# Moving one tile's DMA transposes ahead of the next loads, and its copies of k to other places

## The chip, the cores and the metric

The kernel runs on one core of a Trainium2 chip. The core has five engines that run in parallel, each through its own list of instructions in order: TensorE (PE, with the weight loads PEld beside it), VectorE (DVE), ScalarE (ACT), GpSimd (POOL) and SyncE (SP), which here issues nearly all DMAs. The metric is the device time of one execution in microseconds (us). Lower is better. The kernel before takes 273.0 us, the median of three runs (272.87, 273.00 and 273.41).

## The reference

The program is an attention over chunks of 64 keys, followed by an MLP of two matrix products with an exact GELU between them. Inputs and output are float32.

```python
batch, n_heads, seq, head_dim = 8, 8, 576, 64           # q, k, v
scores = (1 / sqrt(64)) * q_c @ k_c.transpose           # per chunk of 64: q_c, k_c, v_c are (8, 8, 9, 64, 64)
attn   = exp(scores - max) / (sum + 1e-9)
x      = (attn @ v_c), heads side by side               # 4608 tokens x 512
h      = x @ w_in                                       # 512 x 2048
g      = 0.5 * h * (1 + erf(h / sqrt(2)))
out    = g @ w_out                                      # 2048 x 512
```

## The kernel before, in words

**Tiles.** The 4608 tokens are worked in nine tiles of 512. Tile t from 0 to 7 is eight chunks of batch t. Tile 8 is the ninth chunk of all eight batches. While the MLP of tile t runs on TensorE, the attention of tile n = t + 1 is fitted in between, and the loads for tile t + 3 are under way. The loop `for t in range(1, NT)` (L972) sets this up for each t. The constant `T0` (L482) is 3.

**The MLP of a tile.** The first product (`mm1_seven`, L576) makes 16 slots of h. A number in its `order` is one slot made plainly: four 512-column matmuls (L477) and a GELU on ScalarE (L479). Other slots are made in blocks by a scheme with seven products in place of eight (`seven_rows`, L536). The steps p1 to p7 are its products (L551), each of four 256-column matmuls. s11, s12, c22+ are sums or copies between PSUM banks. s12 is `plus(bank["d"], "a")` on VectorE (L555), and the product p4 then accumulates into the same bank d. c11, c12, c22 are GELUs (L559). The scheme needs sums of blocks of x, the four tensor_tensor instructions of `x_sums` (L534): p5 reads the first, p6 the second, p7 the third, p3 the fourth. The second product (`mm2_seven`, L646) also has seven block products, of two half-steps each (14 slots, L706), with sums of blocks of h from `g_sum` (L644 and, for the third, L631).

**The attention of a tile.** q and k arrive in float32 on SP (`load_qk`, L118), GpSimd casts them to bf16 (`pool_cast_qk`, L164), and SP's DMA transposes bring them to the layout that the scores need (`flip`, L194, into q_t and k_t; k_t has one buffer). `k_by_chunk` (L196) then copies k_t in four instructions (L207), one for each pair of heads, to k_c, whose columns stand chunk by chunk; for tile 5 it writes back into that tile's k_nat, which the transpose has read by then. `quad_S` (L233) makes the scores on TensorE (L239) and their exponentials on ScalarE (L246). `quad_sums`, `quad_over`, `att_rc` and `quad_x_plain` form the sums and scale the result of the value product `quad_av` (L334) into x. V is loaded by nine DMAs of a tile on SP (`load_v_rows`, L128) and cast on GpSimd (`cast_v_rows`, L214).

**What sets the order.** Every engine's order is written out by hand. `mm1_seven` walks its `order` list: a step such as "p4" issues its work, and a name or number that has hooks in `extra1` (e1 in the loop) issues those first. `mm2_seven` does the same for its slots with `extra2` (e2). "x" is the place of the x sums and "k" the place of the k copies. `next_loads` (L997) issues, for tile t, the loads and casts of q and k of tile t + 3, and of V of tile t + 2. A DMA on SP waits in line behind all earlier ones, and SP often runs behind the other engines.

In the kernel before, the loop of tile 2 issues `next_loads` first (q and k of tile 5, V of tile 4). The transposes of tile 4 come at the first slot of the second product:

```python
            if t == T0:
                flip(n + 1, "q")
            elif t > 1:
                next_loads()
```

In the loop of tile 3 the copies of tile 4's k stand at "k", behind p3. The transpose of tile 5's k and `next_loads` stand ahead of slot 9, and the copies of tile 5's k (VectorE, all four) ahead of slot 15. The scores of both tile 4 and tile 5 are made in the second product of tile 3 (slots 0 and 10).

Of the kernel before, what the change touches and what calls it, by code (L numbers as in the profile page):

```python
# [11 lines left out]
def kernel(  # L12
# [178 lines left out]
    def flip(t, nm):  # L191
        st = tiles[t]
        st[nm + "t"] = flips.tile([P, G * J, P], bf16, tag=nm + "t", name=f"{nm}_t", bufs=2 if nm == "q" else 1)
        nc.sync.dma_start_transpose(st[nm + "t"][:], st[nm][:].rearrange("p g j r d -> p (g j r d)"))  # L194

    def k_by_chunk(t, copy, gs=range(G)):  # L196

        st = tiles[t]
        if t == K0:
            st["kc"] = st["kt"][:].rearrange("p (g n) (c e) -> p g (n c) e", g=G, c=2)  # L200
            return
        if "kc" not in st and t == T0 + 2:
            st["kc"] = st["k"][:].rearrange("p g j r d -> p (g j r d)").rearrange("p (g i e) -> p g i e", g=G, i=CT)
        elif "kc" not in st:
            st["kc"] = flips.tile([P, G, CT, CH], bf16, tag="kc", name="k_c", bufs=1)
        for g in gs:
            copy(st["kc"][:, g].rearrange("p i (c j) -> p i c j", j=J),  # L207
                 st["kt"][:, g * J:(g + 1) * J].rearrange("p j (i c) -> p i c j", i=CT))
# [108 lines left out]
    def quad_over(t, m):  # L317

        rb, r1 = tiles[t]["rb"], tiles[t]["r1"]
        for s in range(G):  # L320
            nc.scalar.copy(rb[QD * s:QD * (s + 1), m], r1[QD * m:QD * (m + 1), (m % 2) ^ (s // 2)])
# [108 lines left out]
    DV, AC, PO = nc.vector.tensor_copy, nc.scalar.copy, nc.gpsimd.tensor_copy  # L430
# [51 lines left out]
    T0 = 3  # L482
# [93 lines left out]
    def mm1_seven(t, hooks):  # L576

        if t > 1:
            tiles[t]["h"] = hpool.tile([P, FF, MT], bf16, tag="h", name="h")
        kept = [work.tile([P, HM, HD], f32, tag="t1", name="kept_p5", bufs=2)[:] for _ in range(2 if t in TWICE else 1)]  # L580
        bank, more = {}, {}
        if t == 1:
            does = seven_rows(t, 1, {"a": TP, "b": AT, "d": AT}, kept[0], bank)
        else:
            does = seven_rows(t, 0, {"a": AT, "b": AT, "d": AT}, kept[0], bank)
        if t in TWICE:
            does.update((step + "'", do) for step, do in
                        seven_rows(t, 1, {"a": TP, "b": TP}, kept[1], more).items())
            fifth = does["p5'"]
            does["p5'"] = lambda: (more.update(d=bank["b"]), fifth())  # L590
        if t == NT - 1:
            order = ("p1", "s11", "p1'", "s11'", "p5", 8, "p2", "c11", "p6", 9, "s12", "p5'", "p6'", "s12'", 10, "p7", "p4",
                     "c22+", "c12", "c22", "p7'", 11, "p3", "p2'", "c11'", "c22+'", "p4'", "c22'", 12, "c12'", "p3'", 13,
                     "g0", 14, "s3", 15)
        elif t > T0 + 1:
            order = ("p1", "p1'", "s11", "t0", "s11'", 8, "p2", "p2'", "c11", "p5", "p6", "p5'", "p6'", "c11'", "s12", 9, 10,
                     "s12'", "p7", "p4", "c22+", "p7'", "c22+'", "t1", "p4'", "c12", "c22", "p3", 11, "c12'", "c22'", 12, "p3'",
                     13, "g0", 14, "s3", 15)
        elif t == T0 + 1:
            order = (4, 5, 6, "p1", "s11", 7, "p2", "p5", "c11", "p6", 8, "s12", "t0", 9, 10, "p4", "p7", "c12", "c22+",  # L600
                     "t1", 11, "c22", 12, "p3", "g0", 13, "s3", 14, 15)
        elif t == T0:
            order = ("x", "p1", "s11", 4, "p5", "p2", "c11", 5, "p6", "s12", 6, "p4", "p7", "c12", "c22+", 7, "c22", 8, "p3",
                     "k", 9, 10, "s3", 11, 12, 13, "g0", 14, 15)
        elif t == 2:
            order = ("p1", "s11", "p1'", "x", "s11'", 8, "p2", "c11", "p5", 9, "p6", "s12", "p5'", "p6'", "s12'", 10, "p7", 11,
                     "c22+", "c22", "p7'", 12, "p4", "c12", "p3", "c22+'", "p3'", 13, "p4'", "p2'", "k", "c22'", "c11'", "c12'",
                     "g0", 14, 15, "s3")
        else:
            order = (9, "p1", "s11", 10, 11, "w", "p5", "p2", "c11", "p6", 12, "s12", "w0", "p4", "p7", "c12", "c22+", "w1", 13,  # L610
                     "c22", "p3", 14, "g0", "s3", 15)
        for step in order:
            if step in does:
                does[step]()
                continue
            for u in hooks.get(step, ()):
                u()
            if not isinstance(step, str):
                mm1_slot(t, step)
# [187 lines left out]
    def pool_cast_qk(t, names="qk"):  # L807
        for nm in names:
            for g in range(G):
                cast_qk(t, nm, g, PO)  # L810
# [33 lines left out]
    with tc.manual_schedule():  # L844
# [46 lines left out]
        p2 = att_sum_pe(0, 2)  # L891
        p3 = att_sum_pe(0, 3)
# [70 lines left out]
        def flip_qk(t):  # L963
            for nm in "qk":
                flip(t, nm)
# [6 lines left out]
        for t in range(1, NT):  # L972
            n = t + 1
# [35 lines left out]
                    pool_cast_qk(t + 3, "k")  # L1009
            if t == T0:  # L1010
                flip(n + 1, "q")
            elif t > 1:
                next_loads()
            e1, e2 = {}, {}
            exp, gelu = lambda: act_table(Act.Exp), lambda: act_table(Act.Gelu)
# [3 lines left out]
            e1 = {"s3": [lambda: g_sum(t, 3)], "g0": g[0]} if t not in DENSE else {9: [lambda: g_sum(t, 3)], 13: g[0]}  # L1019
            e2 = {0: g[1][:2], 2: g[1][2:]}  # L1020
            if t <= T0:
                ov = [lambda m=m: quad_over(n, m) for m in range(G)]
                rx = [[lambda m=m: att_rc(n, m), lambda m=m: quad_x_plain(n, m)] for m in range(G)]
                e2 = {0: [exp, lambda: quad_S(n, ALONE)] + g[1][:2], 2: g[1][2:],
                      4: [lambda: quad_sums(n)], 5: [ov[0]], 6: [ov[1]],
                      7: [ov[2]] + rx[0], 8: [ov[3]] + rx[1], 9: rx[2], 10: rx[3]}
                e2[{1: 7, 2: 5, T0: 4}[t]].insert(1, lambda: quad_av(n, ALONE))
                if t > 1:
                    e1["x"] = [lambda: x_sums(t)]
                if t == 1:  # L1030
                    e1["w"] = [lambda: weight_sum(2), lambda: weight_sum(3)]
                    e1["w0"] = [lambda: w_in_sums(0, (0, 1))]
                    e1["w1"] = [lambda: w_in_sums(0, (2, 3))]
                    e2[2].append(lambda: weight_sum(4))
                    e2[4].append(lambda: [load_qk(4, nm) for nm in "qk"])
                    e2[7] += [lambda: pool_cast_qk(4), lambda: flip_qk(3), lambda: load_v_rows(3), lambda: cast_v_rows(3, PO)]
                else:
                    e1["k"] = [lambda: k_by_chunk(n, DV)]
                if t < T0:
                    if t > 1:  # L1040
                        e2[0].append(lambda: flip_qk(n + 1))
                    e2[11] = [gelu]
                else:
                    e1[9] = [lambda: flip(n + 1, "k"), next_loads]
                    e1[15] = [lambda: k_by_chunk(n + 1, DV)]
                    e2[10] += [lambda: quad_S(n + 1, BETWEEN), gelu]
                    e2[12] = parts[0]
                    e2[13] = [lambda: x_sums(n)] + parts[1]
            elif n < NT:
                rcs = [lambda m=m: quad_rc(n, m // 2, m % 2) for m in range(G)]  # L1050
                if t == T0 + 1:
                    e1["t0"] = [lambda: quad_total(n, (0,))]
                    e1["t1"] = [lambda: quad_total(n, (1,))] + rcs[1:3]
                else:
                    e1["t0"] = [lambda: quad_totals(n)]
                    e1["t1"] = rcs[1:]
                e2 = {0: [exp, lambda: quad_av(n, ALONE)] + g[1][:2] + xs[:2], 4: xs[2:] + g[1][2:],
                      6: [lambda: x_sums(n, (0, 1))], 10: [lambda: x_sums(n, (2, 3))], 11: [gelu]}
                if t == T0 + 1:
                    e2[2] = rcs[3:]  # L1060
                if n + 1 < NT:
                    for i, gs in enumerate(((0,), (1, 2), (3,))):
                        e2.setdefault(2 * i + 2, []).append(lambda gs=gs: k_by_chunk(n + 1, AC, gs))
                    e2[8] = [lambda: quad_S(n + 1, ALONE)] + parts[0][:1]
                    e2[10] += parts[0][1:] + parts[1]
# [29 lines left out]
```

## Time and profile before

The profile is of one execution on the chip, taken by the hardware profiler. Its times are microseconds from the start of its span.

| what | value |
|---|---|
| median of three runs | 273.0 us (272.87 to 273.41) |
| the profiled execution's own time | 274.27 us |
| its span, first to last instruction | 272.5 us |
| granted TensorE clock | 1.00 |
| TensorE busy | 261.5 us (96%) |
| VectorE busy | 208.1 us (76%) |
| ScalarE busy | 195.1 us (72%) |
| GpSimd busy | 89.6 us (33%) |
| first product of tile 3 | 106.10 to 119.77 |
| second product of tile 3 | 119.77 to 135.35 |

The profiled execution lies 1.27 us over the median. About 1.8 us of its time lie outside the span. An "order of time" below gives start, duration, engine, line, operation, and the tile that is written and the ones that are read; a bracket at the end tells how long the engine was idle before and what ended that. In it the end of a matmul is modelled, and one matmul begins before the one ahead of it has ended, so distances on TensorE are read from start to start. SPq is SP issuing a DMA: its duration is that of the issue, not of the transfer.

### The profile page before, as it was taken

Reading aid. Unit: us, or ns where it says so; the run is one execution under the profiler, and the core shown is the slowest. Engines: PE = TensorE matmul, PEld = TensorE weight load, DVE = VectorE, ACT = ScalarE, POOL = GpSimd, SP = SyncE. Lnnn points to the kernel's source line nnn. Section 1 sums busy time; section 2 is a strip of 40 time slices with the busy share of each in tenths; the row PEclk is TensorE's granted clock in tenths of the full one; section 3 lists DMA queues with packets and bytes.
Section 4 is the critical chain, followed back from the end, with each engine's and each line's share of the span. In section 5 each row is a group of like instructions: output and inputs, shape, how many; then the busy total and the mean of one; then the engine's idle time right before and its main releaser. Section 6 shows DMA issues by size and latency. Waiting matters only on the chain.

```text
span 272.5 us, 7244 instructions
## 1 busy us (share of the span) xinstructions
PE 261.5 (96%) x2913; PEld 192.3 (71%) x2933; DVE 208.1 (76%) x352; ACT 195.1 (72%) x376; POOL 89.6 (33%) x150
## 2 busy tenths in 40 slices
PE   8699999999999999998999999999999999999993
PEld 3378775566876787567855887588758876886682
DVE  6874877989985979578988998888887888635621
ACT  3767758898677967787877967897788779357610
POOL 7869768501284326104534900032400200000000
PEclk9999999999999999999999999999999999999999
DMA  6999999899899897999699327999974220130014
GB/s 206 264 353 404 391 396 227 231 207 250 255 384 229 222 309 173 299 262 286 188 223 349 89 79 186 173 139 166 226 170 99 89 79 2 38 115 2 0 41 117
DMA packets 104738, 53.96 MB, mean 198 GB/s; under 512 B 72960, under 2 KB 101632, under 8 KB 104704
## 3 DMA queue, kind: packets, MB, share of 16 engines
q1 hardware_dynamic: 104400, 53.23, 73.3%
q8 instruction: 23, 0.38, 0.6%
q10 hardware_dynamic: 304, 0.26, 0.3%
q14 instruction: 11, 0.09, 0.1%
HBM read 36.70 MB, written 9.44 MB: 169 GB/s over the span
## 4 chain that ended last, share of the span: by engine, by line
PE 86%; ACT 5%; DMA 4%; SPq 2%; issue 1%; ACTq 0%; DVE 0%; POOL 0%; POOLq 0%
PE y_ps L706 33%; PE h_ps L477 22%; PE hs_ps L551 14%; PE h_ps L451 5%; PE y_ps L778 2%; DMA arrival<-in_moe_w_in_dram 2%; SPq L157 2%; PE av_ps L334 2%; DMA arrival<-in_q_dram 2%; PE h_ps L467 2%; ACT pT L246 1%; PE y_ps L742 1%; PE y_ps L451 1%; PE s_ps L239 1%; ACT L842 1%
## 5 line engine op out<-in xcount | busy, mean ns | idle before, releaser
L477 PE MATMUL h_ps<-x,w_in_sb 128*128 128x512 bf16 x269 | 65.4, 379 | 0.8
L479 ACT ACTIVATE h<-h_ps 128x512 bf16<-128x512 f32 x85 | 50.7, 600 | 19.2 <-PE h_ps L477 14.9
L477 PEld LDWEIGHTS <-w_in_sb 128*128 128x128 bf16 x284 | 27.7, 98 | 25.2
L706 PEld LDWEIGHTS <-h 128*128 128x128 bf16 x384 | 36.9, 98 | 5.0 <-issue 0.2
L164 POOL CAST q_nat<-arrival 128x512 bf16<-128x512 f32 x31 | 20.9, 713 | 58.0 <-DMA arrival<-in_q_dram 32.9
L214 POOL CAST v_nat<-arrival 128x1024 bf16<-128x1024 f32 x14 | 15.2, 1097 | 48.5 <-DMA arrival<-in_v_dram 48.5
L706 PE MATMUL y_ps<-v_bd,k_bd 128*128 128x256 bf16 x256 | 29.8, 273 | 0.8 <-issue 0.7
L706 PE MATMUL y_ps<-w_out_sb,h 128*128 128x256 bf16 x256 | 29.3, 273 | 0.0
L706 PEld LDWEIGHTS <-k_bd 128*128 128x128 bf16 x256 | 24.6, 98 | 4.4 <-issue 0.9
L673 DVE TENSOR_TENSOR kept<-y_ps,kept 128x512 f32<-128x512 f32 (+1 forms) x25 | 16.5, 660 | 12.4 <-PE y_ps L706 8.8
L559 ACT ACTIVATE h<-hs_ps 128x512 bf16<-128x512 f32 x39 | 22.8, 600 | 1.7 <-PE hs_ps L551 1.7
L842 ACT ACT_TABLE_LOAD x18 | 23.1, 1283 | 1.1 <-PEq L1079 0.7
L668 ACT COPY kept<-y_ps 128x512 f32<-128x512 f32 (+1 forms) x26 | 14.5, 557 | 12.7 <-PE y_ps L706 12.5
L164 POOL CAST k_nat<-arrival 128x512 bf16<-128x512 f32 x30 | 19.7, 692 | 7.0 <-DMA arrival<-in_k_dram 6.5
L551 PEld LDWEIGHTS <-w_in_sb 128*128 128x128 bf16 x156 | 15.2, 98 | 5.3 <-issue 0.4
L555 DVE TENSOR_TENSOR hs_ps<-hs_ps,kept_p 128x512 f32<-128x512 f32 x13 | 8.7, 687 | 9.4 <-PE hs_ps L551 7.2
L706 PE MATMUL y_ps<-v_bd,s_sb 128*128 128x256 bf16 x128 | 15.3, 273 | 0.0
L706 PE MATMUL y_ps<-w_out_sb,s 128*128 128x256 bf16 x128 | 15.3, 273 | 0.0
L706 PE MATMUL y_ps<-v_bd,h 128*128 128x256 bf16 x128 | 15.3, 273 | 0.0
L246 ACT ACTIVATE pT<-s_ps 128x512 bf16<-128x512 f32 x28 | 14.4, 603 | 0.7 <-PE s_ps L239 0.7
L451 PE MATMUL h_ps<-x,w_in_sb 128*128 128x256 bf16 x128 | 14.1, 273 | 0.3 <-POOL w_in_sb L823 0.3
L551 PE MATMUL hs_ps<-x,w_in_sb 128*128 128x256 bf16 x104 | 14.3, 273 | 0.0
(138 smaller groups left out, 487.4 us busy)
## 6 DMA issues: line engine op xcount, KB each, us to landing
arrival<-in_v_dram SPq DMA_DIRECT2D x58, 128.0 KB, 4.1
arrival<-in_q_dram SPq DMA_DIRECT2D x7, 1024.0 KB, 7.1
arrival<-in_k_dram SPq DMA_DIRECT2D x6, 1024.0 KB, 10.1
out_dram<-kept SPq DMA_DIRECT2D x21, 256.0 KB, 2.7
arrival<-in_moe_w_out_dram SPq DMA_DIRECT2D x4, 1024.0 KB, 11.6
arrival<-in_moe_w_in_dram SPq DMA_DIRECT2D x6, 512.0 KB, 8.1
out_dram<-y_sb SPq DMA_DIRECT2D x11, 256.0 KB, 2.8
arrival<-in_k_dram SPq DMA_DIRECT2D x8, 256.0 KB, 5.6
```

The source lines that it names most:

```text
L164: copy(st[nm][:, g].rearrange("p j r d -> p r j d"), st[nm + "f"][:, 2 * g:2 * g + 2])
L214: copy(st["v"][:, r::2], st["vf"][:, r::2])
L246: nc.scalar.activation(pT[:].rearrange("p u (c j) -> p u c j", j=J), s_ps[g2][c][:].rearrange("p u (j c) -> p u c j", j=J), Act.Exp, scale ...
L451: nc.tensor.matmul(to[:, cols], left, right[:, cols], start=(start and a == 0), stop=stop, skip_group_check=True)
L477: (nc.tensor.matmul if t else by_halves)(h_ps[:], w_in_sb[:, ks, f * P:(f + 1) * P], tiles[t]["x"][:, ks, :], start=(ks == 0), stop=(ks == ...
L479: nc.scalar.activation(tiles[t]["h"][:, f, :], h_ps[:], Act.Gelu)
L551: nc.tensor.matmul(hs[:, f], left[:, ks, f * P:(f + 1) * P], right[:, ks], start=(fresh and f == 0 and ks == 0), stop=(ks == 1), skip_grou ...
L559: nc.scalar.activation(h[:, n:n + HM, HD * c:HD * (c + 1)], src, Act.Gelu)
L668: nc.scalar.copy(kept[name][:, ms], ps[:])
L673: nc.vector.tensor_tensor(y_sb[:, ms], ps[:], y_sb[:, ms], op=ADD)
L706: nc.tensor.matmul(to, left(f, m), right[:, f], start=(fresh and (split or m == 0) and f == 0), stop=(f == HF - 1), skip_group_check=True)
L842: nc.scalar.activation(act_scratch[:], rest[:, 0:1], func)
```

## The change

In tile 2's loop, the transposes of tile 4's q and k move from the start of the second product to "k" in the first one, behind the copies of tile 3's k, and `next_loads` moves from the start of the loop to the place just behind them. On SP the two transposes thereby stand ahead of the two loads of tile 5's q and k and the nine of tile 4's V; ahead of both stand the same stores as before.

In tile 3's loop, "k" moves from behind p3 to the place right behind "x". So the four copies of tile 4's k follow the x sums on VectorE and stand ahead of s12. The transpose of tile 5's k and `next_loads` also move to that place; on SP their order among the other DMAs stays. The copies of tile 5's k leave slot 15 of the first product. They are issued in slot 2 of the second one, behind the last partial sum: those of heads 4 to 7 on ScalarE, those of heads 0 to 3 on VectorE.

TensorE's and GpSimd's orders stay the same.

```diff
         elif t == T0:
-            order = ("x", "p1", "s11", 4, "p5", "p2", "c11", 5, "p6", "s12", 6, "p4", "p7", "c12", "c22+", 7, "c22", 8, "p3",
-                     "k", 9, 10, "s3", 11, 12, 13, "g0", 14, 15)
+            order = ("x", "k", "p1", "s11", 4, "p5", "p2", "c11", 5, "p6", "s12", 6, "p4", "p7", "c12", "c22+", 7, "c22", 8, "p3",
+                     9, 10, "s3", 11, 12, 13, "g0", 14, 15)
...
             if t == T0:
                 flip(n + 1, "q")
-            elif t > 1:
+            elif t > T0:
                 next_loads()
...
                 else:
-                    e1["k"] = [lambda: k_by_chunk(n, DV)]
+                    e1["k"] = [lambda: k_by_chunk(n, DV), lambda: flip_qk(n + 1) if t < T0 else flip(n + 1, "k"), next_loads]
                 if t < T0:
-                    if t > 1:
-                        e2[0].append(lambda: flip_qk(n + 1))
                     e2[11] = [gelu]
                 else:
-                    e1[9] = [lambda: flip(n + 1, "k"), next_loads]
-                    e1[15] = [lambda: k_by_chunk(n + 1, DV)]
+                    e2[2] += [lambda: k_by_chunk(n + 1, AC, (2, 3))] + [] + [lambda: k_by_chunk(n + 1, DV, (0, 1))]
                     e2[10] += [lambda: quad_S(n + 1, BETWEEN), gelu]
```

## The prediction

> **What bounds the kernel now.** First the page's busy times and its chain that ended last, since they say which engine a microsecond has to be taken from:
>
> ```profile
> PE 261.5 (96%) x2913; PEld 192.3 (71%) x2933; DVE 208.1 (76%) x352; ACT 195.1 (72%) x376; POOL 89.6 (33%) x150
> PE 86%; ACT 5%; DMA 4%; SPq 2%; issue 1%; ACTq 0%; DVE 0%; POOL 0%; POOLq 0%
> ```
>
> TensorE is busy for 261.5 of 272.5 us. No DMA stands on the chain but for the first loads. A transfer or a copy that comes earlier is therefore worth only as much as TensorE waits for it today. Next, the two halves of tile 3, the tile that the change touches most, as stretches (columns: length, then busy time of PE, PEld, DVE, ACT, POOL):
>
> ```profile
> 106.10:119.77 13.67, 13.57 (x77) 7.32 (x77) 9.60 (x15) 10.11 (x18) 3.33 (x4) 1.00 1.07 261
> 119.77:135.35 15.58, 14.88 (x309) 12.69 (x309) 13.41 (x22) 12.46 (x32) 6.60 (x10) 1.00 0.83 237
> ```
>
> In the first product TensorE lacks 0.10 us, in the second 0.70 us. The order of time on TensorE says where:
>
> ```profile
> 109.58 1.03 PE L477 MATMUL h_ps<-x,w_in_sb 128*128 128x512 bf16 x4
> 110.60 0.60 PE L551 MATMUL hs_ps<-x,w_out_sb 128*128 128x256 bf16 x4
> ...
> 127.95 1.58 PE L706 MATMUL y_ps<-v_bd,k_bd 128*128 128x256 bf16 x13 [0.69 <-issue]
> ```
>
> Four 512-column products take 0.86 us from start to start elsewhere (108.28 to 109.14), so p4 at 110.60 starts 0.16 us late. The other gap, 0.69 us, is put down to no engine, semaphore or DMA. So TensorE waits for no transpose and no k copy in tile 3. VectorE does wait for them, as its own order of time shows:
>
> ```profile
> 106.16 0.57 DVE L534 TENSOR_TENSOR k_bd<-x 128x512 bf16<-128x512 bf16 x1
> 106.77 0.72 DVE L534 TENSOR_TENSOR k_bd<-x,k_bd 128x512 bf16<-128x512 bf16 x1
> 107.41 1.25 DVE L534 TENSOR_TENSOR k_bd<-x 128x512 bf16<-128x512 bf16 x1
> 108.58 0.41 DVE L534 TENSOR_TENSOR k_bd<-x,k_bd 128x512 bf16<-128x512 bf16 x1
> 109.84 0.70 DVE L555 TENSOR_TENSOR hs_ps<-hs_ps,kept_p 128x512 f32<-128x512 f32 x1 [0.85 <-PE hs_ps L551]
> 111.67 0.69 DVE L555 TENSOR_TENSOR kept_p<-hs_ps,kept_p 128x512 f32<-128x512 f32 x1 [1.12 <-PE hs_ps L551]
> 113.39 2.14 DVE L207 COPY k_c<-k_t 128x512 bf16<-128x512 bf16 x4 [1.03 <-DMA k_t<-k_nat]
> ```
>
> This is the place that decides. The x sums end at 108.99, and s12 (L555, at 109.84) waited 0.85 us for p6. p4 accumulates into the bank that s12 writes, and p4 starts 0.06 us after s12's end (110.54). So s12 is already on TensorE's path, with 0.85 us of VectorE's idle time ahead of it. The k copies of tile 4 come later, where VectorE is free.
>
> **The change part by part.**
>
> SP, tile 2. Two transposes move ahead of eleven loads: q and k of tile 5 and the nine of tile 4's V. The queue's order of time:
>
> ```profile
> 93.48 0.59 SPq L118 DMA_DIRECT2D arrival<-in_q_dram  x1
> 94.12 0.99 SPq L118 DMA_DIRECT2D arrival<-in_k_dram  x1
> 95.16 12.19 SPq L128 DMA_DIRECT2D arrival<-in_v_dram  x9
> 107.45 1.76 SPq L194 DMA_TRANSPOSE q_t<-q_nat  x1
> 109.32 1.93 SPq L194 DMA_TRANSPOSE k_t<-k_nat  x1
> ```
>
> The casts of tile 4 ended on POOL at 85.3 and the tile-3 copies that free k_t at 89.5, so neither transpose waits at 93.48. They issue at 93.5 and 95.3, and with the 4.0 us from issue to landing of the present k transpose, k_t lands at about 99.4 in place of 113.36. The loads behind them move by 1.76 + 1.93 + two gaps of 0.05 = 3.8 us: q of tile 5 lands at about 104.4 (now 100.64), its k at about 108.4 (now 104.61). Where loads now follow a transpose pair, k lands 10.6 to 12.0 us after the k transpose was issued (138.71 to 149.32; 116.60 to 128.59), which gives 105.9 to 107.3. So k lands between 105.9 and 108.4. V's casts on POOL move from 107.16 and 109.44 to some 111 and 113; the value product that needs them is at 124.34. That costs nothing; without that 10 us of cover, each us would be a us of TensorE.
>
> SP and POOL, tile 3. The transpose of tile 5's k and the loads behind it keep their place on SP: the queue runs behind the program and reaches that transpose at 116.60 now, at some 114 to 117 then. It newly waits only for the early copies of tile 4 to free k_t, by 111.1. No cost. POOL's order is the same.
>
> VectorE, tile 3, k copies of tile 4. Four copies, 0.52 us from start to start (113.39, 113.91), so 2.06 us till the next can start. They move from 113.39 to straight behind the x sums; behind them wait s12, and p4 behind s12. Their data will be there (99.4). s12 then starts at the end of the x sums + 2.06, or at 109.84 if that is later; it can't come sooner, since it waits for p6, so a gain is excluded. What is unknown is the length of the x sums, 2.83 us now, beside POOL's casts. Bounds: 1.57 us (tile 4's four at 136.56 to 138.13, with no cast of 512 elements beside them) gives 106.16 + 1.57 + 2.06 = 109.79, no delay. The present 2.83 us gives 111.05, a delay of 1.21 us. Nearest is tile 2's group, 78.83 to 81.18, 2.35 us, beside q and k casts only, as it will be here: the V cast that stretched the third sum to 1.25 us will lie after it. 106.16 + 2.35 + 2.06 = 110.57, a delay of 0.73 us. I take 0.73.
>
> Whether the copies themselves stretch beside POOL's casts no row shows: all twelve of them on VectorE (0.59 to 0.61 us) ran with POOL idle. Nearest rows: a PSUM sum beside a V cast at 109.84 kept its 0.70; a two-input sum beside one went from 0.42 to 1.25. Below, 0; above, 0.83; I take 0, since the copies read one tensor. [...]
>
> What follows s12 has room: the next sum, c22+, waited 1.12 us for TensorE, and p3, which it lets go, starts 0.83 us after its end (112.36 to 113.19). The place left at 113.39 gains nothing: the sums from 115.44 on end at 119.26, and their next partner is a product at 125.
>
> VectorE and ScalarE, tile 3, k copies of tile 5. Today four on VectorE at 120.42 (2.06 us, 1.16 us of waiting for the transpose ahead of them). Then the partial sums behind them end at 124.61; TensorE reads the second at about 125.5, so it does not wait and gains nothing by their coming 2 us earlier. Two copies then stand on VectorE behind those sums (1.05 us, by about 123.7, ahead of the transpose at 124.53 that waits for TensorE anyway): 0. Two go to ScalarE behind its copy that ends at 124.41. ScalarE's k copies take 1.10 us each (1.0 from start to start, tile 6), so 2.1 us where 1.25 us are idle; its next idle times are 0.46, 0.28 and 0.70. The copy of u2 ends at 128.05 in place of 127.55, the exponentials at 131.71 are on time. TensorE overwrites u2's bank at 129.36. Cost 0; if the cover of 1.3 us went (the 0.69 us stall gone), 0.5 us of cover are left.
>
> Sum: +0.73 against the profiled execution's 274.27 us (272.5 of span), which is 1.27 over the median. TensorE has no slack after tile 3 to win it back: tiles 4 to 7 repeat at some 26.8 to 27.4 us with no wait. Against the median 273.0 that is 273.7.
>
> **The rivals.** (1) *Hidden anyway.* The x sums run beside a gap between the q and the k casts, take 1.6 to 2.1 us, and s12 is late by 0 to 0.5. For it: q's casts may end before 106.16 and k's start after 107.7. Against: both landings are uncertain by more than the gap. Time 273.0 to 273.5, say 273.2.
>
> (2) *Faster: the gap at 127.95 closes.* TensorE's program arrives by DMA in 16 KB pieces. The packet records have one that started at 125.52, just after q of tile 6 had landed (124.64); none had come for 19.6 us before it, the longest pause in the program's body, and nothing else explains the gap. If the loads of tile 6 are issued differently against that piece, the 0.86 us (0.97 between two matmuls instead of 0.11) go. It decides if the piece arrives 0.9 us sooner and s12 is late by under 0.3: 273.0 + 0.2 - 0.86 = 272.3. Against: TensorE's program and SP's order there are unchanged, and the median is already 1.27 under the profiled execution, so unprofiled runs may not have this gap. [...]
>
> (3) *Slower by more.* The same piece waits for k of tile 6 (now landing 128.59, 4 us after q) instead of q, because q's load comes up to 3 us earlier; TensorE then stands for some 1 us more, on top of s12: 274.7.
>
> **How the numbers follow.** A change under 0.2% (0.55 us) can't be told from none here. The forecast, s12 late by 0.55 to 1.25, gets 0.40; rival 1 0.27; rival 2 0.23; rival 3 0.10. Slower: 0.40 + 0.10 = 0.50; within: 0.27; faster: 0.23. The range of 272.2 to 274.7 holds the forecast, rival 1 and about half each of rivals 2 and 3: 0.83.
>
> **What would show it.** In tile 3's first product: k_t landed near 99; four L207 copies directly behind the L534 sums at about 108.5; s12 at about 110.6 with no wait for TensorE; p4 at about 111.3 with a gap of 0.9 us ahead of it; everything after it shifted. Then two L207 copies on ScalarE at about 125 and the u2 copy 0.5 later with no TensorE wait. Wrong if p4 starts within 0.3 us of the end of slot 6's product, which stands ahead of it, or if the gap near 127 to 128 changes by more than the one at p4.

## The result, and the profile after

The changed kernel takes 276.31 us (median of six executions, 275.26 to 277.83), the kernel before 273.21 us beside it. The ratio is 1.0115, with a 95% interval of 1.0082 to 1.0148: slower by 1.2%. The ratios here and below leave out an execution that lies over 1.5% above the fastest one of its kernel. The forecast was 273.7 us, with a range up to 274.7. The direction and the place were right. The size was too small by a factor of four: 3.1 us where 0.7 was forecast.

The profiled execution took 276.97 us, with a span of 275.1 (before: 274.27 and 272.5). The page's busy times and its chain that ended last:

```profile
PE 263.1 (96%) x2913; PEld 193.3 (70%) x2933; DVE 209.1 (76%) x350; ACT 197.0 (72%) x378; POOL 94.1 (34%) x150
PE 84%; ACT 6%; DVE 5%; DMA 2%; issue 1%; SPq 0%; ACTq 0%; POOL 0%; DVEq 0%; POOLq 0%
```

VectorE, 0% of the chain before, now holds 5% of it. In tile 3 that is the last two k copies and s12 (110.00 to 112.54). A longer piece lies in tile 4 (147.07 to 156.59), but TensorE shows no wait there, and tile 4 takes only 0.31 us longer than before (27.69 instead of 27.38). POOL is busy 4.5 us longer with the same 150 instructions. That is the first sign of what went wrong. The two halves of tile 3 (length, then busy time of PE, PEld, DVE, ACT, POOL, the granted clock of TensorE, the DMA share and GB/s):

```profile
105.45:123.44 17.99, 15.25 (x78) 7.93 (x77) 11.04 (x15) 10.19 (x18) 8.37 (x10) 0.91 0.97 252
123.44:138.17 14.73, 14.73 (x310) 12.72 (x309) 13.02 (x20) 14.28 (x34) 8.74 (x10) 1.00 0.62 175
```

The first product takes 17.99 us where it took 13.67, and its clock is 0.91. The second takes 14.73 where it took 15.58. TensorE's order of time shows the one wait:

```profile
108.92 1.03 PE L477 MATMUL h_ps<-x,w_in_sb 128*128 128x512 bf16 x4
112.59 0.80 PE L551 MATMUL hs_ps<-x,w_out_sb 128*128 128x256 bf16 x4 [2.64 <-DVE hs_ps L555]
113.18 1.06 PE L551 MATMUL hs_ps<-k_bd,w_out_sb 128*128 128x256 bf16 x4
```

p4 waits 2.64 us for s12 (L555). VectorE's order of time shows why s12 is late, and GpSimd's shows what ran beside it:

```profile
105.51 0.46 DVE L534 TENSOR_TENSOR k_bd<-x 128x512 bf16<-128x512 bf16 x1
106.01 0.71 DVE L534 TENSOR_TENSOR k_bd<-x,k_bd 128x512 bf16<-128x512 bf16 x1
106.65 0.82 DVE L534 TENSOR_TENSOR k_bd<-x 128x512 bf16<-128x512 bf16 x1
107.40 0.82 DVE L534 TENSOR_TENSOR k_bd<-x,k_bd 128x512 bf16<-128x512 bf16 x1
108.15 3.78 DVE L207 COPY k_c<-k_t 128x512 bf16<-128x512 bf16 x4
111.85 0.68 DVE L555 TENSOR_TENSOR hs_ps<-hs_ps,kept_p 128x512 f32<-128x512 f32 x1
```

```profile
105.09 2.86 POOL L164 CAST q_nat<-arrival 128x512 bf16<-128x512 f32 x4 [10.65 <-DMA arrival<-in_q_dram]
107.91 3.58 POOL L164 CAST k_nat<-arrival 128x512 bf16<-128x512 f32 x4
111.43 2.39 POOL L214 CAST v_nat<-arrival 128x1024 bf16<-128x1024 f32 x2
```

The four k copies take 3.78 us where they took 2.14, and the four k casts beside them 3.58 where four casts take 2.29 alone. They alternate, one copy and one cast, each holding up the other: copies start at 108.15, 109.07, 110.00 and 110.92, casts at 107.91, 108.64, 109.59 and 110.51.

A second thing follows the wait. The trace's clock records have the granted clock at 0.5 from 112.84 to 116.26, 3.41 us. As stretches of TensorE (same columns as above):

```profile
112.50:113.50 1.00, 0.91 (x6) 0.70 (x6) 0.03 (x1) 0.08 (x1) 1.00 (x2) 0.67 0.99 339
113.50:114.50 1.00, 1.00 (x6) 0.54 (x5) 0.22 (x1) 0.52 (x1) 0.32 (x1) 0.50 0.98 312
116.50:117.50 1.00, 1.00 (x8) 0.62 (x7) 0.00 (x0) 1.00 (x3) 0.00 (x0) 1.00 1.24 279
```

While the clock is at 0.5, a 512-column matmul takes 427 ns from start to start; at 1.0 it takes 216.

So the two profiled executions differ like this, start to start on TensorE: from the start to tile 3, -0.65; from tile 3's start to p4, 7.14 instead of 4.50, +2.64; from p4 to the first score matmul, 10.85 instead of 9.17, +1.68 (the clock); tile 3's second product, -0.85 (the gap of before is not there); the rest, -0.22. The sum is the +2.6 of span.

### The profile page after: what moved, and what is told of

Same layout as the page of the kernel before. It is cut to its first block, busy times and chain, and to the rows that moved or that the text cites. A ratio compares the mean times of both kernels' runs of the same rounds, so it can differ in the third digit from the quotient of the medians.

```text
span 275.1 us, 7244 instructions
## 1 busy us (share of the span) xinstructions
PE 263.1 (96%) x2913; PEld 193.3 (70%) x2933; DVE 209.1 (76%) x350; ACT 197.0 (72%) x378; POOL 94.1 (34%) x150
## 4 chain that ended last, share of the span: by engine, by line
PE 84%; ACT 6%; DVE 5%; DMA 2%; issue 1%; SPq 0%; ACTq 0%; POOL 0%; DVEq 0%; POOLq 0%
PE y_ps L706 32%; PE h_ps L477 21%; PE hs_ps L551 15%; PE h_ps L451 5%; PE y_ps L778 2%; DMA arrival<-in_k_dram 2%; ACT k_bd L188 2%; PE h_ps L467 2%; ACT pT L246 1%; PE av_ps L334 1%; DVE k_bd L644 1%; PE y_ps L742 1%; PE y_ps L451 1%; PE s_ps L239 1%; ACT L842 1%
## 5 line engine op out<-in xcount | busy, mean ns | idle before, releaser
L477 PE MATMUL h_ps<-x,w_in_sb 128*128 128x512 bf16 x269 | 66.5, 384 | 0.8
L164 POOL CAST q_nat<-arrival 128x512 bf16<-128x512 f32 x31 | 22.2, 753 | 59.9 <-DMA arrival<-in_q_dram 59.9
L214 POOL CAST v_nat<-arrival 128x1024 bf16<-128x1024 f32 x14 | 17.0, 1227 | 45.2 <-DMA arrival<-in_v_dram 45.2
L164 POOL CAST k_nat<-arrival 128x512 bf16<-128x512 f32 x30 | 21.5, 750 | 3.6 <-DMA arrival<-in_k_dram 3.4
L644 DVE TENSOR_TENSOR k_bd<-h 128x1024 bf16<-128x1024 bf16 x16 | 12.5, 779 | 5.6 <-ACT h L479 5.6
L555 DVE TENSOR_TENSOR hs_ps<-hs_ps,kept_p 128x512 f32<-128x512 f32 x13 | 8.7, 685 | 9.6 <-PE hs_ps L551 7.9
L551 PEld LDWEIGHTS <-w_out_sb 128*128 128x128 bf16 x112 | 11.2, 100 | 6.6 <-issue 2.9
```

The source lines that it names most:

```text
L164: copy(st[nm][:, g].rearrange("p j r d -> p r j d"), st[nm + "f"][:, 2 * g:2 * g + 2])
L214: copy(st["v"][:, r::2], st["vf"][:, r::2])
L477: (nc.tensor.matmul if t else by_halves)(h_ps[:], w_in_sb[:, ks, f * P:(f + 1) * P], tiles[t]["x"][:, ks, :], start=(ks == 0), stop=(ks == ...
L551: nc.tensor.matmul(hs[:, f], left[:, ks, f * P:(f + 1) * P], right[:, ks], start=(fresh and f == 0 and ks == 0), stop=(ks == 1), skip_grou ...
L644: nc.vector.tensor_tensor(st["S", i][part], a, b, op=op)
```

## The experiments

After the result the theory was: the whole loss is the k copies of tile 4 standing ahead of s12, stretched by GpSimd's casts, with a halved TensorE clock behind the wait in some executions. Rivals were: the later loads of tile 2 (A), ScalarE's copies (B), copies that are slow for another reason than casts (C), a clock that falls for another reason than the wait (D).

### Only the place of the k copies undone

```diff
-            order = ("x", "k", "p1", "s11", 4, ..., 8, "p3", 9, 10, ...)
+            order = ("x", "p1", "s11", 4, ..., 8, "p3", "k", 9, 10, ...)
```

(against the changed kernel; the list is otherwise the same. The transpose of tile 5's k and `next_loads`, which are issued at "k" too, move back with the copies.)

> The changed kernel with one step undone: in tile 3 the k step goes back behind p3. The transposes of tile 4 stay early, tile 5's k copies stay in the second product on ScalarE and VectorE. Theory (the loss is the k copies of tile 4 standing ahead of s12 on VectorE, stretched by GpSimd's casts, and a halved TensorE clock after the wait): the loss is gone, 273.2 us give or take 0.5, s12 waits for TensorE again, p4 less than 0.3 us late, granted clock 1.0 throughout. Rival A (the loads of tile 5 and V of tile 4 coming 3.8 us later cost it): stays at 275 to 276. Rival B (ScalarE's 2 us of k copies in the second product cost it): stays at 275 to 276.

Measured: 272.77 us, ratio to before 0.9988 (0.9965 to 1.0012). VectorE's order of time:

```profile
109.11 0.70 DVE L555 TENSOR_TENSOR hs_ps<-hs_ps,kept_p 128x512 f32<-128x512 f32 x1 [1.02 <-PE hs_ps L551]
110.94 0.69 DVE L555 TENSOR_TENSOR kept_p<-hs_ps,kept_p 128x512 f32<-128x512 f32 x1 [1.12 <-PE hs_ps L551]
111.55 2.98 DVE L207 COPY k_c<-k_t 128x512 bf16<-128x512 bf16 x4
```

s12 waits for TensorE again, by 1.02 us, and p4 is 0.16 us late, as before the change. One copy of the four, beside a cast of V, takes 1.45 us in this trace, and nothing waits for it. The whole loss goes with this one step, so rivals A and B fall.

### Only the tile 2 part

```diff
-            elif t > 1:
+            elif t > T0:
                 next_loads()
...
-                    e1["k"] = [lambda: k_by_chunk(n, DV)]
+                    e1["k"] = [lambda: k_by_chunk(n, DV)] + ([lambda: flip_qk(n + 1), next_loads] if t < T0 else [])
...
-                    if t > 1:
-                        e2[0].append(lambda: flip_qk(n + 1))
```

(against the kernel before)

> The kernel before with the tile 2 part of the change alone: transposes of tile 4 ahead of the loads; tile 3 wholly as before. Theory: 273.2 us give or take 0.5, since nothing on TensorE waits for what moves. Rival A (the later loads and casts): 275 or more. Rival B: 273.2 here, and e_kback slow.

Measured: 273.43 us, ratio 1.0011 (0.9991 to 1.0032). In tile 3 TensorE waits only for the same 0.16 us ahead of p4. That the loads come later, behind the transposes, costs nothing that can be measured.

### Only tile 5's copies

```diff
-                    e1[15] = [lambda: k_by_chunk(n + 1, DV)]
+                    e2[2] += [lambda: k_by_chunk(n + 1, AC, (2, 3)), lambda: k_by_chunk(n + 1, DV, (0, 1))]
```

(against the kernel before)

> The kernel before with the last part of the change alone: tile 5's k copies in the second product of tile 3, two on ScalarE and two on VectorE. Theory: no difference from the kernel before, 273.2 us give or take 0.5; ScalarE's copy of u2 comes about 0.5 us later and TensorE doesn't wait for it. Rival B (they cost): 273.8 or more, with a gap ahead of the sixth block product.

Measured: 272.80 us, ratio 0.9979 (0.9956 to 1.0002). No cost, and no gain that the interval shows. ScalarE's two copies take 2.20 us and its copy of u2 follows later, as worked out; TensorE shows no wait there.

### Only the early place, without the early transposes

```diff
-            order = ("x", "p1", "s11", 4, ..., 8, "p3", "k", 9, 10, ...)
+            order = ("x", "k", "p1", "s11", 4, ..., 8, "p3", 9, 10, ...)
...
-                    e1["k"] = [lambda: k_by_chunk(n, DV)]
+                    e1["k"] = [lambda: k_by_chunk(n, DV)] + ([lambda: flip(n + 1, "k"), next_loads] if t == T0 else [])
...
-                    e1[9] = [lambda: flip(n + 1, "k"), next_loads]
```

(against the kernel before)

> The kernel before with the k step of tile 3 moved behind the x sums and nothing else: the transposes of tile 4 stay behind the loads and land near 113.4. Theory: the copies wait for them with s12 and p4 behind, s12 starts at about 113.4 + 2.1 = 115.5 in place of 109.8, TensorE waits 5 to 6 us ahead of p4 and its clock falls: 273 + 5.7 + 1.7 = 280 us, at least 278. Rival E (SP's order is of no account, since something else holds the copies): 276, as the changed kernel.

Measured: 280.76 us, ratio 1.0261 (1.0221 to 1.0302). VectorE's order of time, then TensorE's:

```profile
111.71 2.09 DVE L207 COPY k_c<-k_t 128x512 bf16<-128x512 bf16 x4 [4.50 <-DMA k_t<-k_nat]
113.72 0.69 DVE L555 TENSOR_TENSOR hs_ps<-hs_ps,kept_p 128x512 f32<-128x512 f32 x1
```

```profile
114.46 1.01 PE L551 MATMUL hs_ps<-x,w_out_sb 128*128 128x256 bf16 x4 [4.86 <-DVE hs_ps L555]
```

Without the early transposes VectorE stands 4.50 us waiting for k_t with s12 behind it, and TensorE 4.86 us. Here GpSimd had nothing to cast at the time and the copies take 2.09 us. So the early place needs the tile 2 part, by which k_t landed at 101.06 in the changed kernel, against some 111.7 here. What that part doesn't bring is a silent GpSimd.

### GpSimd's casts moved away from the copies, in two steps

First, in tile 2, the casts of tile 5's k behind those of V; then those of q as well. Both are against the changed kernel.

```diff
-                late = t + 3 == NT - 1
+                late = t + 3 in (5, NT - 1)
```

> The changed kernel, with one change to GpSimd's order: in tile 2 its casts of tile 5's k stand behind its casts of tile 4's V instead of ahead of them. Theory (the copies of k on VectorE are stretched by the casts that run beside them): GpSimd is idle from about 108.2 till V lands near 111, so the four copies run at about 0.52 us apart, 2.1 us in place of 3.7; s12 is 1.0 to 1.2 us late in place of 2.6; TensorE's wait ahead of p4 is about 1.1 us and too short for the clock to fall; 274.2 to 274.7 us. Rival C (the copies are slow for another reason, such as the loads landing in SBUF at that time): copies still 0.9 us apart, 276 us.

```diff
+                if t == 2:
+                    for nm in "qk":
+                        load_qk(t + 3, nm)
+                    load_v_rows(n + 1)
+                    cast_v_rows(n + 1, PO)
+                    pool_cast_qk(t + 3)
+                    return
                 late = t + 3 == NT - 1
```

> The changed kernel, with GpSimd's order altered once more: in tile 2 both tile 5's q and k are cast behind tile 4's V, so that GpSimd has nothing to cast from tile 3's cast of V (about 94) till V of tile 4 lands (about 108 to 111). Theory: the x sums take 1.6 us and the four k copies 2.1 us, s12 starts within 0.2 us of p6's end, the wait ahead of p4 is no longer than the 0.16 us of the kernel before, and the time is 273.0 us give or take 0.5, although the copies still stand ahead of s12. Rival C (the place alone costs, whatever GpSimd does): p4 1 us or more late, 274 or more. Tile 5's transposes come some 3 us later by this; if that reaches TensorE, a gap appears in the second product of tile 3.

The first: 274.11 us, ratio 1.0035 (1.0009 to 1.0062). In its profiled execution q landed late, so its casts, not k's, ran beside the first two copies. One trace thus has both cases: copies one and two start 0.92 us apart and take 1.00 and 1.01 us beside casts; the last two, with GpSimd idle, start 0.50 us apart and take 0.58. Transfers went on all that time (266 GB/s during the first two copies, 196 during the last two; 307 during the copies of the next run, which are not stretched), so rival C falls. The wait ahead of p4 was 1.46 us, where about 1.1 was expected, since two copies were still stretched.

The second: 273.74 us, ratio 0.9992 (0.9970 to 1.0014; the kernel before took 273.41 us beside it). VectorE's order of time in it:

```profile
107.38 0.42 DVE L534 TENSOR_TENSOR k_bd<-x,k_bd 128x512 bf16<-128x512 bf16 x1
107.72 2.15 DVE L207 COPY k_c<-k_t 128x512 bf16<-128x512 bf16 x4
109.94 0.70 DVE L555 TENSOR_TENSOR hs_ps<-hs_ps,kept_p 128x512 f32<-128x512 f32 x1
```

The copies stand ahead of s12 and cost nothing: x sums 1.54 us, copies 2.15, p4 0.16 us late as in the kernel before. The place alone is harmless; place and casts together make the loss. Its profiled execution (275.3 us, 1.6 over its median) also shows the debt of moving the casts. Tile 5's transposes come later, ScalarE's k copies wait for k_t, and the copy of u2 behind them is late, so TensorE waits in the second product (TensorE's order of time):

```profile
130.59 1.91 PE L706 MATMUL y_ps<-v_bd,s_sb 128*128 128x256 bf16 x16 [1.82 <-ACT kept L668]
```

### Copies of 127 rows in place of 128

```diff
+            for g in gs:
+                to = st["kc"][:, g].rearrange("p i (c j) -> p (i c) j", j=J)
+                of = st["kt"][:, g * J:(g + 1) * J].rearrange("p j m -> p m j")
+                copy(to[:, 0:P - 1], of[:, 0:P - 1])
+            copy(st["kc"][:, :, CT - 1].rearrange("p g (c j) -> p g c j", j=J)[:, :, PC - 1],
+                 st["kt"][:].rearrange("p (g j) m -> p g j m", g=G)[:, :, :, P - 1])
```

(in `k_by_chunk`, for tile 4 alone, against the changed kernel. The source of a whole copy runs over 128 rows of 4, its destination over one run of 512; here it is 127 rows against 508.)

> The changed kernel, with tile 4's four k copies cut to 127 of 128 rows of four elements (508 of 512 elements) and the remaining 16 elements of all of them copied by one small instruction. All else as in the changed kernel, GpSimd's casts included. [...] Rival G (any copy with an SBUF input contends): still 0.9 us apart, casts 0.98 us.

Measured: 275.81 us, ratio 1.0082 (1.0049 to 1.0114). VectorE's order of time, then GpSimd's:

```profile
108.13 3.85 DVE L210 COPY k_c<-k_t 128x508 bf16<-128x508 bf16 x4
111.90 0.47 DVE L211 COPY k_c<-k_t 128x16 bf16<-128x16 bf16 x1
112.29 0.69 DVE L563 TENSOR_TENSOR hs_ps<-hs_ps,kept_p 128x512 f32<-128x512 f32 x1
```

```profile
105.82 2.86 POOL L164 CAST q_nat<-arrival 128x512 bf16<-128x512 f32 x4 [11.74 <-DMA arrival<-in_q_dram]
108.63 2.29 POOL L164 CAST k_nat<-arrival 128x512 bf16<-128x512 f32 x4
```

The k casts beside these copies take 2.29 us, 0.61 each, as if alone, where they took 3.58 beside whole copies. So these copies don't hold the casts up, and rival G, with its casts of 0.98 us, falls. But the copies did not get shorter: the three that began beside casts took 1.02 to 1.05 us, the last one, with GpSimd idle, 1.01, and they came 0.93 to 0.96 us apart. The whole copies are thus the quicker ones (0.52 us apart when GpSimd is idle) and the ones that contend; a copy of 508 elements is slow by itself, for a reason that no run shows. Either way s12 comes about as late (the wait for it was 3.11 us here), so nothing is won.

### TensorE kept busy in the wait

```diff
-            order = ("x", "k", ..., "s12", 6, "p4", ...)
+            order = ("x", "k", ..., "s12", 6, "warm", "p4", ...)
...
+                    e1["warm"] = [lambda: keep_warm(8)]
```

(against the changed kernel; measured in two sets, the second together with the changed kernel itself)

> The changed kernel with eight matmuls of no use (128x512, 1.7 us in all) on TensorE right ahead of p4, where it waits 2.6 us for s12. They do not touch the result. Theory: p4 starts no later, the clock stays at 1.0 in every execution, and the time is 275.3 us give or take 0.4, with no execution near 277; the halved clock is then worth about 1.7 us of the executions that have it. Rival D (the halved clock is not set off by this wait): executions near 277 with the clock at 0.5 for 3.4 us stay, 276.3.

> The changed kernel once more, next to the following run. Theory on the clock: executions fall in two groups, near 275.4 with the clock at full rate through tile 3 and near 277.3 where it is halved for 3.4 us after the wait ahead of p4; the median lies between, 276.2. Rival D (no link of the clock with this wait): the same share of low mean clocks as in the kernel before.

> The changed kernel with eight matmuls of no use in the wait ahead of p4, which do not touch the result, once more next to the run of the changed kernel. Theory on the clock: no group near 277.3 beyond the share of slow ones of the kernel before, median 275.4, that is 0.6 to 1.0 us under the changed kernel in the same rounds. Rival D: no difference between the two.

Measured: with the extra matmuls 275.70 and 275.80 us (ratios 1.0103, 1.0067 to 1.0139, and 1.0082, 1.0054 to 1.0111); the changed kernel again 276.44 us (1.0096, 1.0064 to 1.0128). The stretches of the two kernels around the wait and behind it, first the changed kernel's second profile, then the one with the extra matmuls:

```profile
111.00:113.50 2.50, 0.23 (x2) 0.00 (x0) 2.48 (x4) 0.60 (x1) 2.50 (x4) 1.00 0.74 165
113.75:117.00 3.25, 3.25 (x13) 1.66 (x11) 0.69 (x1) 0.60 (x1) 2.20 (x3) 0.50 0.91 286
```

```profile
110.30:112.70 2.40, 1.90 (x9) 0.78 (x8) 2.40 (x3) 0.60 (x1) 1.97 (x2) 1.00 0.94 297
112.78:116.00 3.22, 3.22 (x21) 2.05 (x21) 0.69 (x1) 1.88 (x4) 0.25 (x1) 1.00 1.19 158
```

In both profiles of the changed kernel the half clock begins within 0.3 us of the end of the wait, while the traces with the wait filled have it nowhere in the kernel's body (mean clocks 1.000 and 0.999). The shares of executions with a low mean clock say the same: 0.994 or less in 10 of 18 of the changed kernel, in 2 of 12 with the extra matmuls, and in 16 of 73 of the kernel before. Both speak against rival D, that the fall has nothing to do with this wait. In the times the effect is small. The medians are 0.6 us lower with the extra matmuls both times, the ratios by only 0.0012 and 0.0014, with intervals that overlap. And one part of the expectation failed: each set has an execution over 277 us (277.51 at a mean clock of 0.999, 277.18 at 0.991), the first of which no clock explains.

### Two repeats

The kernel before, for a second profile, and the first experiment with more executions:

> The kernel before, once more, for one more profile. Theory on the gap of 0.69 us in the second product of tile 3 (at 127.95 in the first profile): if it is a matter of when TensorE's program arrives, it need not come back; without it tile 3 takes 28.4 us and not 29.25 from its first product to tile 4's, and the span is about 271. If it belongs to the order of the work, it is there again at the same matmul.

> The changed kernel with the k step of tile 3 back behind p3, once more, to tell it from the kernel before. Theory: TensorE waits nowhere in tile 3 for longer than 0.16 us in either, so 272.9 us give or take 0.4, no difference that can be measured; at most the 0.1 to 0.3 us that VectorE's and SP's waits of the kernel before could have cost in some executions.

The kernel before took 273.84 us in its one execution, and the gap of 0.69 us is not there. TensorE's order of time shows all 32 matmuls in one piece, where the first profile was cut after 19:

```profile
125.41 3.67 PE L706 MATMUL y_ps<-v_bd,k_bd 128*128 128x256 bf16 x32
```

So the gap belonged to one execution, not to the order of work. The piece of the program that came at 125.52 in the first profile came at 124.66 here, while the matmuls around it ran 0.41 us later. That fits the argument that a late piece made the gap, but it is one execution of each kind, and no run shows the cause. The kernel with only the place undone took 273.07 us, ratio 0.9983 (0.9966 to 1.0000). It is the quickest of the versions with early transposes, and faster than the changed kernel by some 1.2%, but not clearly faster than the kernel before.

## Why the prediction was right or wrong

**What bounds, right.** TensorE waited for no transpose in tile 3, so the early transposes could gain nothing, and they gained nothing (1.0011). s12 was the place that decides.

**SP and POOL in tile 2, right.** k_t landed at 101.06 (worked out: 99.4), q of tile 5 at 104.97 (104.4), its k at 107.79 (105.9 to 108.4), and V's casts came at 111.43 and 112.78 (111 and 113). k_t came 1.7 us later than worked out, still 7 us ahead of its first copy. No cost, as the experiment with this part alone shows.

**The length of the x sums, nearly right.** 2.64 us from the first sum to the first copy; 2.35 was taken. 0.29 us too short. The row that it was taken from, tile 2's group, has a pause of GpSimd in it (79.36 to 80.26); here q's casts ran through.

**The k copies, wrong: this step failed.** The prediction took 2.06 us for the four and said of their stretching beside GpSimd's casts "I take 0, since the copies read one tensor", with 0.83 us as the upper end. Measured: 3.70 us from the first copy to s12, +1.64. Two errors lie in it. The value was taken from rows in which GpSimd was idle, as its order of time in the kernel before shows around the copies at 113.39 and at 120.42:

```profile
109.44 1.04 POOL L214 CAST v_nat<-arrival 128x1024 bf16<-128x1024 f32 x1 [1.06 <-DMA arrival<-in_v_dram]
124.77 2.29 POOL L164 CAST q_nat<-arrival 128x512 bf16<-128x512 f32 x4 [14.28 <-DMA arrival<-in_q_dram]
```

And the upper end counted one stretched instruction, when each of the four stands beside a cast of its own and grows by 0.41 us. With the measured terms the step's own sum is 0.73 + 0.29 + 1.64 = 2.66, and the wait in the profile is 2.64 us.

The 0 us for the stretching rested on the copies' reading one tensor, and no run shows that this keeps a copy clear of a cast. Whole copies and casts hold each other up (copies 0.92 us apart, casts 0.98 us long), while the copies of 508 elements leave the casts alone (0.61 us). Both read one tensor; what makes the difference, no run shows.

**The clock, missed altogether.** Neither the sum nor a rival had it: 1.68 us in the profiled execution. In the 18 executions of the changed kernel, ten have a mean clock of 0.994 or less. The eight others average 275.0 us, nine of the ten 277.2 (the tenth took 278.9). Such means also come from a fall in the first 20 us, as the second profiles of the kernel before and of the changed kernel show (mean clocks 0.991 and 0.984), and 16 of 73 executions of the kernel before have them. So they don't count the falls in tile 3; the traces place one there in both profiles of the changed kernel. With a mean clock above 0.994 the changed kernel is still some 1.9 us slower (275.0 against 273.1 for the kernel before). That is the wait for s12, which was 2.64 and 2.30 us in the two profiles; whether it is shorter in those eight executions, no trace shows.

**What follows s12, right.** c22+ waited 1.75 us for TensorE, and the sums behind it were in time.

**Tile 5's copies, right.** ScalarE's two copies took 2.13 us, the copy of u2 ended 0.8 us ahead of the matmuls that overwrite its bank (131.38 and 132.18), and TensorE didn't wait; alone they cost nothing (0.9979). The two on VectorE were stretched by casts as well, 1.95 us for the two, and were hidden.

**The rivals.** Rival 1 (x sums short, copies hidden) is what came when GpSimd was silent: 0.9992. Its condition was right, its place among the casts was not. Rival 2 (the gap closes) did happen in the profiled execution, -0.85 us, but the gap is not there in the second profile of the kernel before either, so it was no gain. Rival 3 (274.7) had the right sign, but its mechanism, a wait of TensorE for a piece of the program, did not come: TensorE waits nowhere in the second product of tile 3.

## What to carry to other kernels

Before an instruction of VectorE is moved ahead of one that TensorE waits for, look at what GpSimd does at the new place, not at the old one, and price each of the moved instructions beside it. The rows with the neighbour idle were the lower end here: 2.14 us for the four copies against 3.78 beside casts. The wait of TensorE of 2.64 us cost its own length and then 1.68 us by the clock, while behind the one of 1.46 us (late k casts) the clock stayed at 1.0. By these numbers the author's estimate is that two waits of 1.4 us in different windows of the table below would cost 2.8 us, less than the 4.3 of the one of 2.64; that was not run.

## What the runs showed of the hardware that was not expected

**Copies and casts hold each other up, at 0.93 us a pair.** Alone, a k copy comes every 0.52 us and a cast every 0.56. Beside each other, both come every 0.93 us, in three traces (the changed kernel twice, and the first two copies of the run with late k casts). That is less than the 1.08 us of one after the other. A copy of 508 elements in 127 rows comes every 0.93 to 0.96 us, but leaves the casts at 0.56.

**Changes of the granted clock lie whole multiples of 3.413 us apart.** In the first profile of the changed kernel the clock records are 105.81 us at 1.0 (31 times 3.413), 3.413 us at 0.5, 157.01 us at 1.0 (46 times) and a last one at 0.5 from 273.27 on; in that of the kernel before, 266.24 us at 1.0 (78 times) and a last one at 0.5 from 272.73 on. The first record begins 7.03 us from the start of the span in the one and 6.49 in the other, so the phase differs from one execution to the next. Cut from these changes on into windows of 3.413 us, each trace gives the idle time of TensorE inside a window (from its modelled ends) and what the clock did in the window after it:

| run | window | idle in it, us | clock in the next window |
|---|---|---|---|
| changed kernel | 109.43 to 112.84 | 2.64 | 0.5 |
| changed kernel, second profile | 110.30 to 113.71 | 2.30 | 0.5 |
| early place, late transposes | 108.38 to 111.79 | 2.19 | 0.5 |
| the same, next window | 111.79 to 115.21 | 2.67 | 0.5 |
| odd copies | 108.39 to 111.80 | 1.88 | 1.0 |
| odd copies, next window | 111.80 to 115.22 | 1.23 | 1.0 |
| silent GpSimd, second product | 128.51 to 131.92 | 1.82 | 1.0 |
| late k casts | 109.69 to 113.11 | 1.46 | 1.0 |

The wait of 3.11 us with odd copies is the longest but one and left the clock alone; the border at 111.80 cuts it into 1.88 and 1.23. The wait of 2.30 us lay inside one window, and the clock fell. In these rows 2.19 us idle and more stand ahead of a clock of 0.5, and 1.88 and less ahead of 1.0. The ends of the two first profiles agree: 2.44 us idle (changed kernel, 269.86 to 273.27) and 3.41 (kernel before, 269.31 to 272.73) stand ahead of 0.5, 1.52 (kernel before, 265.90 to 269.31) ahead of 1.0. In the first 20 us it is different: the clock fell to 0.5 there after windows with only 1.28, 1.50 and 1.86 us idle (the changed kernel's second profile, the late k casts, the second profile of the kernel before), and stayed at 1.0 after one with 1.67 (the silent GpSimd). So idle time alone doesn't decide it, and what does is open.
